# Four 32x32 transposes of beta moved up in VectorE's queue

## The chip, the cores and the metric

One Trainium2 chip, one of its cores. The metric is the device time of one execution in microseconds (us). Three runs of the kernel before took 374.45, 374.64 and 375.24 us; the median is 374.64.

## The reference

Sigmoid attention over 8 batches, 12 heads, 448 positions and 64 features per head, and behind it a feed-forward layer whose activation is `h * sigmoid(beta * h)`, with one `beta` for each of the 2048 hidden features:

```
def _attn_ref(q, k, v):
    S = q.shape[2]
    scale = 1.0 / np.sqrt(q.shape[-1])
    scores = scale * np.matmul(q, k.transpose(0, 1, 3, 2)) - np.log(S)
    attn = 1.0 / (1.0 + np.exp(-scores))
    return np.matmul(attn, v).astype(np.float32)

def _moe_ref(x, w_in, w_out, beta):
    h = x @ w_in
    g = h * (1.0 / (1.0 + np.exp(-beta * h)))
    return (g @ w_out).astype(np.float32)
```

`x` is the attention's output as 3584 rows of 768; `w_in` is 768 x 2048, `w_out` 2048 x 768. The kernel takes and gives float32 and multiplies in float16.

## The kernel before

**The steps.** A *group* is four heads of one batch, so a batch has three groups. For a group, `load_one` (L126) brings q and k into `raw`, GpSimd issuing the load; VectorE transposes 32x32 blocks into `qT` (L208) and `kT` (L217, L221). TensorE multiplies them into score tiles in PSUM (`score`, L237), and ScalarE turns a score tile into weights `attns` (L250 for one tile, L265 for two at once). TensorE multiplies the weights with `v` (`attend`, L340), and VectorE casts the result into `xT` (L349). Then comes the first layer (`dense1`, L362): six products with `w_in` make one column block `dc` of h; ScalarE takes its sigmoid with a column of `beta_sb` as scale (L374), and VectorE multiplies (L377). The second layer (L392) writes the output through `osb`. Later windows of the work use sums of blocks in Strassen's manner (L531, L651, L445); they are the same in both kernels.

**The order.** Nothing is scheduled by a planner: the program's order is each engine's order. The first 50 us are written out by hand in the list `BEGIN`, and each engine takes its own instructions out of that list in their order:

- `("q", g, half)` and `("k", g)`: VectorE's transposes of group g (a half of q is 224 of the 448 positions).
- `("scores", g, half, second)`: the scores of group g for one half of the queries (`half_visit`). `second` 0 takes key tiles 0 and 1, `second` 1 the rest. Each entry is 16 products on TensorE into two score tiles, and behind them two activations on ScalarE.
- `("v", 0)`: a copy on VectorE (L171) of the last part of v of batch 0.
- `("values", g, half)`: 16 products (L340) and two casts (L349) for group g.
- `("dense", n)`: the next n products of the list `fill`, here products of the first layer for batch 0.
- `("idle", n)`: n products of zeros (L820) whose result nobody reads.
- `("beta",)`: `beta_columns`, four transposes on VectorE (L834) that turn the sixteen rows of 128 in `beta_in` into columns in `beta_sb`. SyncE loads `beta_in` (L822) at the start, behind a memset on VectorE (L815).

**Score tiles.** At first there are three score tiles, each of two PSUM banks (`share_psum(3)`), and they are taken in turn, two for an entry. Counted from the first entry of scores, tile numbers are 0 1, 2 0, 1 2, 0 1, 2 0, 1 2, 0 1, 2 0, 1 2; after `("two",)` there are two tiles. Where `second` is 0, the order of the 16 products is: two into the first tile, two into the second, and so on. So the third product of `("scores", 0, 1, 0)`, which is the seventh entry and has tiles 0 and 1, needs tile 1 to be free, and tile 1 was filled last by `("scores", 2, 0, 1)`, whose first activation empties it.

```
        def beta_columns():
            ready.add("beta")
            for i in range(P // BLK):
                part = slice(i * BLK, (i + 1) * BLK)
                nc.vector.transpose(out=beta_sb[part], in_=beta_in[:, part])
```

Of the kernel before, what the change touches and what calls it, by code (L numbers as in the profile page):

```python
# [13 lines left out]
def kernel(  # L14
# [70 lines left out]
    def bank(cols: int = S, hold=None, at=None):  # L85
        if at is None:
            at = min((i for i in used if i not in held.values()), key=used.get)
        assert at not in held.values()
        touch(at)
        if hold is not None:  # L90
            held[hold] = at
        width[at] = cols
        return ps[:, at, 0:cols]
# [669 lines left out]
    with tc.manual_schedule():  # L763
# [52 lines left out]
        idle = bank(512)  # L816
# [13 lines left out]
        def beta_columns():  # L830
# [5 lines left out]
        BEGIN = [  # L836
            ("cast", 1, 0, 8, False), ("cast", 1, 8, 14, True), ("cast", 0, 0, 7, True), ("k", 0), ("q", 0, 0),
            ("q", 1, 0), ("idle", 20), ("scores", 0, 0, 1), ("k", 1), ("idle", 1), ("idle", 4), ("idle", 2),
            ("k", 2), ("q", 2, 0), ("scores", 1, 0, 0), ("idle", 9), ("v", 0), ("scores", 1, 0, 1),
            ("scores", 0, 0, 0), ("idle", 7), ("scores", 2, 0, 0), ("values", 0, 0), ("q", 1, 1),  # L840
            ("scores", 2, 0, 1), ("beta",), ("q", 0, 1), ("values", 1, 0), ("scores", 0, 1, 0),
            ("values", 2, 0), ("scores", 0, 1, 1), ("dense", 6), ("scores", 1, 1, 1), ("two",), ("dense", 9),
            ("loads",), ("scores", 1, 1, 0), ("q", 2, 1), ("dense", 21), ("scores", 2, 1, 0), ("dense", 12),
            ("values", 0, 1), ("scores", 2, 1, 1), ("values", 1, 1), ("values", 2, 1), ("dense", 45), ("k", 3),
# [182 lines left out]
```

## Time and profile before

| | |
|---|---|
| median of three runs | 374.64 us (374.45 to 375.24) |
| the profiled execution | 374.53 us, of which its span is 372.8 us |
| TensorE busy | 366.1 us, 98% of the span |
| ScalarE busy | 260.0 us, 70% |
| VectorE busy | 254.4 us, 68% |
| GpSimd busy | 90.4 us, 24% |
| granted TensorE clock, mean | 0.999 |

The profile is of one execution. Times in it are us from the span's start, of which 1.73 us of the execution lie outside (374.53 less 372.8). In a row of the timeline the columns are start, duration, engine, line, operation, result and operands with their shapes, the count of merged instructions, and in brackets the engine's idle time before them with the one that ended it. Merged rows hold instructions that overlap a little, so a sum of means can exceed a row's duration. PE is TensorE, DVE is VectorE, ACT is ScalarE, POOL is GpSimd, SP is SyncE, and PEld is TensorE's loading of weights.

### The profile page before, as it was taken

The numbers are of one execution on the slowest core, as the hardware profiler recorded it, in microseconds if no ns is written. First come the engines' busy times: TensorE is split into PE (matmuls) and PEld (weight loads), VectorE is DVE, ScalarE is ACT, GpSimd is POOL, SyncE is SP. The second block draws the span as 40 slices with busy tenths as digits, with TensorE's granted clock in tenths as the row PEclk, the third lists the DMA queues.
The fourth block names the chain that finished last, engine by engine and source line by source line (L and its number), as shares of the span: only waits on it lengthen the run. The fifth ranks groups of instructions, "written<-read, shape, count | busy, mean of one in ns | idle before, by whom it ended". The sixth has DMA issues, their size and how long they took to land.

```text
span 372.8 us, 7315 instructions
## 1 busy us (share of the span) xinstructions
PE 366.1 (98%) x2907; PEld 185.1 (50%) x2907; DVE 254.4 (68%) x479; ACT 260.0 (70%) x311; POOL 90.4 (24%) x136
## 2 busy tenths in 40 slices
PE   8899999999999999999999999999999999999996
PEld 5466544443444455544444445554444455555664
DVE  4335786776586966787666767778767667679671
ACT  5995766698967668887777749887678647883000
POOL 7833343141151013234133003235100002230000
PEclk9999999999999999999999999999999999999999
DMA  9999999993369030029829410018903111000333
GB/s 171 177 195 203 198 204 198 218 124 51 51 85 174 1 86 1 2 49 128 165 38 218 103 24 21 3 30 113 164 4 86 42 44 42 3 0 1 86 84 128
DMA packets 42546, 34.65 MB, mean 93 GB/s; under 512 B 21888, under 2 KB 38928, under 8 KB 42512
## 3 DMA queue, kind: packets, MB, share of 16 engines
q0 software_dynamic: 36688, 22.47, 44.5%
q1 hardware_dynamic: 5824, 11.71, 10.9%
q8 instruction: 23, 0.38, 0.4%
q14 instruction: 11, 0.09, 0.1%
HBM read 45.62 MB, written 11.01 MB: 152 GB/s over the span
## 4 chain that ended last, share of the span: by engine, by line
PE 89%; ACT 5%; DVE 2%; DMA 1%; issue 1%; POOL 0%; ACTq 0%; POOLq 0%
PE ps L531 26%; PE ps L651 25%; PE ps L237 11%; PE ps L340 10%; PE ps L362 9%; PE ps L392 4%; PE ps L445 4%; ACT attns L265 2%; ACT attns L250 2%; DMA raw<-in_k_dram 1%; ACT sg L374 1%; DVE xT L349 0%; DVE qT L208 0%; DVE kT L217 0%; ACT osb L672 0%
## 5 line engine op out<-in xcount | busy, mean ns | idle before, releaser
L265 ACT ACTIVATE attns<-ps,nlogs 128x1792 f16<-128x1792 f32 x75 | 131.7, 1756 | 41.1 <-PE ps L237 40.1
L651 PEld LDWEIGHTS <-sum 128*128 128x128 f16 x440 | 40.4, 98 | 37.0 <-issue 12.1
L545 POOL TENSOR_TENSOR gt<-attns,sg 128x448 f16<-128x448 f32 x21 | 23.9, 1139 | 141.6 <-ACT sg L542 141.6
L237 PE MATMUL ps<-qT,kT 32*128 32x448 f16 (+3 forms) x864 | 52.3, 341 | 2.1 <-ACT attns L250 1.1
L542 ACT ACTIVATE sg<-ps,beta_sb 128x448 f32<-128x448 f32 x72 | 45.3, 633 | 8.4 <-PE ps L531 5.9
L531 PE MATMUL ps<-xT,w_in 128*128 128x448 f16 x216 | 49.2, 353 | 0.0
L531 PE MATMUL ps<-xT,w_S 128*128 128x448 f16 x216 | 49.2, 352 | 0.0
L651 PE MATMUL ps<-w_T,sum 128*128 128x384 f16 x264 | 48.5, 327 | 0.0
L545 DVE TENSOR_TENSOR gt<-ps,sg 128x448 f16<-128x448 f32 x72 | 44.3, 619 | 3.9 <-ACT sg L542 3.7
L349 DVE CAST xT<-ps 128x448 f16<-128x448 f32 (+1 forms) x54 | 28.9, 568 | 19.8 <-PE ps L340 19.8
L531 PEld LDWEIGHTS <-w_in 128*128 128x128 f16 x288 | 28.0, 98 | 26.6 <-issue 0.7
L340 PE MATMUL ps<-attns,v 128*64 128x448 f16 (+3 forms) x432 | 40.6, 340 | 0.1
L669 DVE TENSOR_TENSOR osb<-ps,osb 128x384 f32<-128x384 f32 x55 | 30.5, 555 | 14.4 <-PE ps L651 12.6
L362 PE MATMUL ps<-xT,w_in 128*128 128x448 f16 (+1 forms) x240 | 39.8, 316 | 0.1
L638 DVE TENSOR_TENSOR sum<-gt 128x1024 f16<-128x1024 f16 x55 | 36.5, 680 | 0.2
L377 DVE TENSOR_TENSOR gt<-ps,sg 128x448 f16<-128x448 f32 (+1 forms) x40 | 20.0, 528 | 22.6 <-ACT sg L374 22.5
L126 POOL DMA_DIRECT2D raw<-in_q_dram x26 | 14.5, 560 | 81.0 <-DVE kT L221 75.1
L651 PE MATMUL ps<-w_out,gt 128*128 128x384 f16 x176 | 33.4, 327 | 0.0
L651 PE MATMUL ps<-w_out,sum 128*128 128x384 f16 x176 | 32.2, 327 | 0.0
L591 DVE TENSOR_TENSOR ps<-ps,attns 128x448 f32<-128x448 f32 x24 | 15.2, 633 | 23.3 <-PE ps L531 20.0
L531 PEld LDWEIGHTS <-w_S 128*128 128x128 f16 x216 | 21.1, 98 | 19.4
L362 PEld LDWEIGHTS <-w_in 128*128 128x128 f16 x240 | 21.9, 98 | 16.8 <-issue 5.6
(54 smaller groups left out, 377.0 us busy)
## 6 DMA issues: line engine op xcount, KB each, us to landing
out_dram<-osb SPq DMA_DIRECT2D x100, 96.0 KB, 2.2
raw<-in_k_dram POOLq DMA_DIRECT2D x23, 224.0 KB, 5.6
raw<-in_q_dram POOLq DMA_DIRECT2D x21, 224.0 KB, 3.8
v<-in_v_dram POOLq DMA_DIRECT2D x32, 144.0 KB, 6.2
w_in<-in_moe_w_in_dram POOLq DMA_DIRECT2D x8, 384.0 KB, 10.4
w_out<-in_moe_w_out_dram POOLq DMA_DIRECT2D x4, 768.0 KB, 13.8
v<-in_v_dram POOLq DMA_DIRECT2D x16, 48.0 KB, 6.1
out_dram<-osb SPq DMA_DIRECT2D x2, 384.0 KB, 2.3
```

The source lines that it names most:

```text
L237: nc.tensor.matmul(sco[base : base + nk, hh, u0 : u0 + n], kT[g][lo : lo + BLK, jt * P : jt * P + nk, e], qT[g][lo : lo + BLK, c0 : c0 + n ...
L265: nc.scalar.activation(out=attns[:, slot : slot + 2].rearrange("p n h s -> p (n h) s"), in_=sco, func=AF.Sigmoid, bias=nlogs[:, 0:1], scal ...
L340: nc.tensor.matmul(av[hh * D : (hh + 1) * D, 0:n], vs[b][base : base + nk, 2 * (s % NPAIR) + hh, jt], at[base : base + nk, hh, 0:n], start ...
L349: nc.vector.tensor_copy(out=xTs[b][:, s % NPAIR, c0 : c0 + n], in_=av[:, 0:n])
L362: nc.tensor.matmul(m1, w_in16[:, hc, dc * P : (dc + 1) * P], xTs[b][:, hc, c0 : c0 + n], start=(hc == 0), stop=(hc == NHC - 1),)
L377: nc.vector.tensor_tensor(out=gt[:, dc, off : off + n], in0=m1, in1=sg[:, 0:n], op=ALU.mult)
L531: nc.tensor.matmul(out, w[:, c, i * P : (i + 1) * P], m[:, c], start=(start and c == 0), stop=(c == KH - 1), skip_group_check=not start,)
L542: nc.scalar.activation(out=sg, in_=h, func=AF.Sigmoid, bias=0.0, scale=beta_sb[:, dc : dc + 1])
L545: return lambda: engine.tensor_tensor(out=gt[:, dc, b % 2 * S : b % 2 * S + S], in0=h, in1=sg, op=ALU.mult)
L638: nc.vector.tensor_tensor(out=sums[t, i], in0=x, in1=y, op=op)
L651: nc.tensor.matmul(m2, (x if op is None else sums[t, i])[:, dc], w[:, dc], start=first, stop=(dc == ND - 1), skip_group_check=i >= 4,)
L669: nc.vector.tensor_tensor(out=out, in0=in0, in1=in1, op=op)
```

## The change

One entry of the list moves. `("beta",)` stood behind the second scores of group 2, between the transposes `("q", 1, 1)` and `("q", 0, 1)` in VectorE's order. It now stands behind the first scores of group 1; in VectorE's order that is behind `("q", 2, 0)` and ahead of the copy `("v", 0)`. No instruction is added or removed, and the order on TensorE, ScalarE, GpSimd and SyncE is the same.

```
         BEGIN = [
...
-            ("k", 2), ("q", 2, 0), ("scores", 1, 0, 0), ("idle", 9), ("v", 0), ("scores", 1, 0, 1),
+            ("k", 2), ("q", 2, 0), ("scores", 1, 0, 0), ("beta",), ("idle", 9), ("v", 0), ("scores", 1, 0, 1),
             ("scores", 0, 0, 0), ("idle", 7), ("scores", 2, 0, 0), ("values", 0, 0), ("q", 1, 1),
-            ("scores", 2, 0, 1), ("beta",), ("q", 0, 1), ("values", 1, 0), ("scores", 0, 1, 0),
+            ("scores", 2, 0, 1), ("q", 0, 1), ("values", 1, 0), ("scores", 0, 1, 0),
             ("values", 2, 0), ("scores", 0, 1, 1), ("dense", 6), ("scores", 1, 1, 1), ("two",), ("dense", 9),
...
```

More of the change, by code (lines that the diff above doesn't have):

```diff
@@ L838 @@
             ("q", 1, 0), ("idle", 20), ("scores", 0, 0, 1), ("k", 1), ("idle", 1), ("idle", 4), ("idle", 2),
-            ("k", 2), ("q", 2, 0), ("scores", 1, 0, 0), ("idle", 9), ("v", 0), ("scores", 1, 0, 1),
+            ("k", 2), ("q", 2, 0), ("scores", 1, 0, 0), ("beta",), ("idle", 9), ("v", 0), ("scores", 1, 0, 1),
             ("scores", 0, 0, 0), ("idle", 7), ("scores", 2, 0, 0), ("values", 0, 0), ("q", 1, 1),
-            ("scores", 2, 0, 1), ("beta",), ("q", 0, 1), ("values", 1, 0), ("scores", 0, 1, 0),
+            ("scores", 2, 0, 1), ("q", 0, 1), ("values", 1, 0), ("scores", 0, 1, 0),
             ("values", 2, 0), ("scores", 0, 1, 1), ("dense", 6), ("scores", 1, 1, 1), ("two",), ("dense", 9),
```

## The prediction

> **What bounds the kernel now.** I read the page first, then busy time by stretches, the waits of TensorE, and then the chain of waits around the moved instructions.
>
> ```profile
> span 372.8 us, 7315 instructions
> PE 366.1 (98%) x2907; PEld 185.1 (50%) x2907; DVE 254.4 (68%) x479; ACT 260.0 (70%) x311; POOL 90.4 (24%) x136
> ...
> 13.50:17.00 3.50, 3.04 (x58) 1.73 (x56) 2.57 (x10) 3.50 (x5) 3.50 (x6) 1.00 1.38 182
> ...
> 45.00:100.00 55.00, 55.00 (x471) 23.88 (x464) 39.60 (x69) 44.19 (x38) 16.00 (x28) 1.00 0.93 149
> ...
> PE ps L820 <- DVE still L814: 1.2, 1, 1.2
> PE ps L237 <- ACT attns L250: 1.1, 3, 0.6
> PE ps L237 <- DVE qT L208: 0.5, 1, 0.5
> PE ps L237 <- DVE kT L217: 0.3, 1, 0.3
> ```
>
> In the stretches the columns behind the length are busy PE, PEld, DVE, ACT, POOL, then the granted clock. TensorE is the bound: busy for 98% of the span, and for 55.00 of 55.00 us from 45 to 100. At the start it is ScalarE's turn: from 13.5 to 17 ACT is busy for all 3.50 us and PE for 3.04. So a microsecond won there counts at the end only if it makes ScalarE, and TensorE behind it, earlier; later, with TensorE full, only a transfer or its own order could take it back. The last four rows are the whole list of waits of TensorE's products (us in total, times, longest): it waits once for a transposed q, for 0.5 us, and for no transfer. The chain of waits shows where:
>
> ```profile
> 15.39 0.32 DVE qT L208
> 15.71 0.08 DVE beta_sb L834
> ...
> 16.23 0.20 DVE beta_sb L834
> ...
> 16.47 0.42 DVE qT L208
> ...
> 16.94 0.63 PE ps L237 x16
> 17.57 1.80 ACT attns L250 x2
> ```
>
> The transposes of beta stand on the chain that ended last, ahead of a q that TensorE wants. That q is `("q", 0, 1)`, and the waiting products are `("scores", 0, 1, 0)`.
>
> **The change part by part: what goes.** VectorE's and TensorE's own rows around that place:
>
> ```profile
> 9.17 0.37 DVE L208 STREAM_TRANSPOSE qT<-raw 128x224 f32<-128x224 f32 x1
> 13.49 0.35 DVE L171 COPY v<-v 64x768 f16<-64x768 f16 x1 [3.95 <-DMA v<-in_v_dram]
> ...
> 15.31 0.40 DVE L208 STREAM_TRANSPOSE qT<-raw 128x224 f32<-128x224 f32 x1
> 15.63 0.80 DVE L834 STREAM_TRANSPOSE beta_sb<-beta_in 32x32 f32<-32x32 f32 x4
> 16.47 0.41 DVE L208 STREAM_TRANSPOSE qT<-raw 128x224 f32<-128x224 f32 x1
> 16.80 0.65 DVE L349 CAST xT<-ps 128x224 f16<-128x224 f32 x2
> ...
> 15.49 0.98 PE L340 MATMUL ps<-attns,v 128*64 128x224 f16 x16
> 16.94 0.58 PE L237 MATMUL ps<-qT,kT 32*128 32x224 f16 x16 [0.46 <-DVE qT L208]
> ```
>
> Without beta the transpose of q can start at 15.63, behind the one of 15.31, instead of 16.47: 0.84 us earlier, done at 16.04. But TensorE is busy with `("values", 1, 0)` until 15.49 + 0.98 = 16.47, so of the 0.84 us at most its own wait of 0.46 is to be had.
>
> Is the q there by 15.63, and what is late next? The load's issue (GpSimd, with the us to landing from the list of issues for that moment), and ScalarE's rows:
>
> ```profile
> 10.13 0.53 POOL L126 DMA_DIRECT2D raw<-in_q_dram  x1 [0.21 <-issue]
> raw<-in_q_dram POOLq DMA_DIRECT2D x1, 112.0 KB, 4.7
> ...
> 10.42 1.01 ACT L250 ACTIVATE attns<-ps,nlogs 128x896 f16<-128x896 f32 x1
> 11.48 0.57 PE L237 MATMUL ps<-qT,kT 32*128 32x224 f16 x14 [0.63 <-ACT attns L250]
> ...
> 15.62 1.53 ACT L250 ACTIVATE attns<-ps,nlogs 128x896 f16<-128x896 f32 x2
> 16.52 0.63 ACT L250 ACTIVATE attns<-ps,nlogs 128x448 f16<-128x448 f32 x1
> 17.55 3.41 ACT L250 ACTIVATE attns<-ps,nlogs 128x896 f16<-128x896 f32 x4 [0.40 <-PE ps L237]
> ```
>
> The q lands at 10.13 + 4.7 = 14.83, 0.80 ahead of 15.63. Next to be late is the score tile. The third product of the entry needs the tile that the activation of 15.62 empties. The pattern is seen once whole in this stage: the activation of 10.42 ends at 11.43, and 14 products, all but the two that fitted the free tile, start 0.05 later and take 0.57. An activation of the same size from 15.62 ends at 15.62 + 1.01 = 16.63, so the 14 start at 16.68 and are done at 17.25. Before, they were done at 16.94 + 0.58 = 17.52. That is **0.27 us earlier**, not 0.46. ScalarE is free at 16.52 + 0.63 = 17.15, so its next activation moves from 17.55 to 17.28, and 0.13 of its idle 0.40 stays.
>
> The bounds of this term: 0.46 if the tile comes free for nothing, zero if something else stops TensorE there. I take 0.27, because the row of 11.48 is the same wait on the same kind of tile.
>
> From 17.28 on the stage is a relay between ScalarE and TensorE. The next products to wait for a tile are those of `("scores", 1, 1, 1)`:
>
> ```profile
> 20.48 0.70 PE L237 MATMUL ps<-qT,kT 32*128 32x224 f16 x14 [0.29 <-ACT attns L250]
> ```
>
> They wait for an activation of the same unbroken ScalarE row that began at 17.55, so they move by the same 0.27. The two casts, at 16.80 only since they stood behind q, go back to about 16.5, so the PSUM banks of `("values", 2, 0)` come free in time for its start at about 17.2.
>
> **What is added.** The four transposes now start behind the q of 9.17, at 9.54, and end at 9.54 + 0.84 = 10.38. Behind them in VectorE's queue is the copy of v, which waits for its own load until 13.49: 3.11 us of cover. Four instructions in idle time are costed at nothing; without that cover they would cost 0.84. The wait that moves with them is for `beta_in`:
>
> ```profile
> 1.65 0.43 SPq L822 DMA_DIRECT2D beta_in<-in_moe_beta_dram  x1
> ...
> beta_in<-in_moe_beta_dram SPq DMA_DIRECT2D x1, 8.0 KB, 4.0
> ```
>
> It lands at 5.65, 3.89 us before its new use. Queued behind it are the copy of v, the casts of values and two transposes of q; who waits for these is TensorE with `("values", 0, 0)` from 13.57. No DMA moves in any queue.
>
> **GpSimd beside it.** In their new place the transposes run while GpSimd issues loads (10.13, then eight of `w_in` from 11.13).
>
> ```profile
> 11.13 6.58 POOL L177 DMA_DIRECT2D w_in<-in_moe_w_in_dram  x8 [0.47 <-DMA v<-in_v_dram]
> ...
> L177 POOL DMA_DIRECT2D w_in<-in_moe_w_in_dram x8: 828/844/871, 11.1 to 16.8; - x8
> ```
>
> In the old place they ran beside the issues of `w_in`, and the longest of the eight took 871 ns against a median of 844: no hold is to be seen, so I cost nothing; held for all of the transposes, the issue of 10.13 would start at 10.38 instead, q land at 15.08, and the sum stay. The Trainium skill ("SBUF — State Buffer", SBUF: two separate sides) says that VectorE and GpSimd share a pair of SBUF ports, that an instruction of VectorE which takes both locks GpSimd out of writing DMA descriptors, and that an issue of some 620 ns took some 3100 ns beside such a copy. By that figure, as an estimate, the issue would end 2.48 us later and the sum would be a loss of 0.84 us (rival C) instead of a gain of 0.27.
>
> **Does the 0.27 us arrive?** Then TensorE needs `w_in` 0.27 us sooner. GpSimd's waits show when parts of it landed at the latest:
>
> ```profile
> 19.66 0.55 POOL L126 DMA_DIRECT2D raw<-in_k_dram  x1 [1.40 <-DMA w_in<-in_moe_w_in_dram]
> ...
> 23.69 0.88 POOL L185 DMA_DIRECT2D w_out<-in_moe_w_out_dram  x1 [1.14 <-DMA w_in<-in_moe_w_in_dram]
> ...
> 21.11 1.11 PE L362 MATMUL ps<-xT,w_in 128*128 128x224 f16 x9
> ...
> 25.57 1.31 PE L362 MATMUL ps<-xT,w_in 128*128 128x224 f16 x12
> ```
>
> The second load (column blocks 2 and 3) is there by 19.66 and first used after six of the nine products of 21.11, so at 21.11 + 6/9 of 1.11 = 21.85; the fourth (blocks 6 and 7) is there by 23.69 and used at 25.57. Both have about 2 us. Sum: nothing added, 0.27 gone: 374.53 - 0.27 = 374.26 us against the profiled execution. That execution is 0.11 below the median of the three runs, so against the median it is 374.64 - 0.27 = **374.37, say 374.4 us**, 0.07% faster. About 0.2%, 0.75 us, is what a measurement of this kernel can tell from no change, so I forecast "within".
>
> **The rivals.**
>
> A. The whole of beta comes off the path. The chain of waits carries it by name, and VectorE's part of it is 16.47 - 15.63 = 0.84 us: 374.53 - 0.84 = 373.69, faster by 0.22%. For it: the ends of TensorE's products are modelled, so the 16.47 at which it is free, and with it the cap of 0.46, is less sure than VectorE's rows. Against it: the activation of 16.52 ends at 17.15, so ScalarE, which is full from 13.5, can't win over 0.40. Chance 0.23.
>
> B. Nothing arrives: the gain is swallowed on the way, by a tile, a bank or a transfer that is as late as before. 374.5. Against it stand the 2 us of `w_in` and the unbroken ScalarE row. Chance 0.13.
>
> C. The transposes hold GpSimd back at 10.13. The q of 15.63 lands late by the hold. Up to 0.80 us that costs nothing, and at 16.47 - 14.83 = 1.64 us all is as before; from there each us costs one. Slower by over 0.75 us needs a hold of 2.39, three times the four transposes; a hold of 2.48 gives 374.53 + 0.84 = 375.37. The page of the Trainium skill named above is the ground for such a size; the eight issues of `w_in` that lay beside the same instructions don't bear it out. Chance 0.07.
>
> D. On the slower side by the moved wait: beta's load is late in the executions that are timed. The place is VectorE's queue ahead of the copy of v; it decides from a landing at 13.49 - 0.84 = 12.65, 7.0 us later than here, and then costs one for one.
>
> ```profile
> w_out<-in_moe_w_out_dram POOLq DMA_DIRECT2D x4, 768.0 KB, 13.8
> ```
>
> If it took as long as the loads of `w_out`, it would land at 1.65 + 13.8 = 15.45, 2.80 too late: 374.53 + 2.80 = 377.3. Against it: it is 8 KB against 768. Chance 0.07.
>
> **How the numbers follow.** The forecast has 0.50, B 0.13 and both lie within 0.2%, less 0.02 for a gain that a measurement lifts over the limit: same 0.61. A, with those 0.02: faster 0.25. C and D: slower 0.14. The range goes down to A, 373.69, and a little under it for the 0.08 us by which the lowest run lies under the profiled one: 373.6. Up it goes to B as the highest of the three runs had it, 375.24: 375.3. C and D, 0.14, lie outside.
>
> **What would show it.** In the changed kernel the four rows of L834 start near 9.5 with no idle time ahead of them; the copy of v stays at 13.49; the q of 16.47 starts at 15.63; TensorE's wait for L208 of 0.5 is gone, and in its place stands a wait of about 0.2 for ACT L250; the ScalarE row of 17.55 starts near 17.28 with 0.13 idle ahead of it; every later row up to 100 us is 0.27 earlier. I am wrong if the first products behind `("values", 1, 0)` wait for something else, if the copy of v is later than 13.5, if the issue of 10.13 takes much over 0.53, or if the rows are 0.27 earlier at 20 and not at 45.

## The result and the profile after

The changed kernel took 374.39 us (median of 21 runs, 374.07 to 375.37); the kernel before, in 21 runs beside it, 375.03 us (374.41 to 376.85). The ratio is 0.9983 with a 95% interval of 0.9975 to 0.9990: faster by 0.17%. The profiled execution took 374.09 us, its span 372.3 us; the one profiled before took 0.44 us more (374.53).

VectorE's and TensorE's timelines of the changed kernel around the moved instructions:

```profile
9.64 0.81 DVE L834 STREAM_TRANSPOSE beta_sb<-beta_in 32x32 f32<-32x32 f32 x4
13.72 0.35 DVE L171 COPY v<-v 64x768 f16<-64x768 f16 x1 [3.27 <-DMA v<-in_v_dram]
14.65 0.69 DVE L349 CAST xT<-ps 128x224 f16<-128x224 f32 x2 [0.58 <-PE ps L340]
15.26 0.69 DVE L208 STREAM_TRANSPOSE qT<-raw 128x224 f32<-128x224 f32 x2
16.46 0.69 DVE L349 CAST xT<-ps 128x224 f16<-128x224 f32 x2 [0.51 <-PE ps L340]
...
15.44 0.99 PE L340 MATMUL ps<-attns,v 128*64 128x224 f16 x16
16.36 0.84 PE L237 MATMUL ps<-qT,kT 32*128 32x224 f16 x16
17.13 0.99 PE L340 MATMUL ps<-attns,v 128*64 128x224 f16 x16
```

Beta runs where VectorE had nothing to do, the two transposes of q stand together, and TensorE's wait for the second is gone. Before, the held products started at 16.94; now they start at 16.36, as soon as the values ahead of them are issued. ScalarE's timelines show what that is worth, the kernel before first and then the changed one:

```profile
8.62 8.54 ACT L250 ACTIVATE attns<-ps,nlogs 128x896 f16<-128x896 f32 x10 [0.29 <-PE ps L237]
```

```profile
8.57 11.99 ACT L250 ACTIVATE attns<-ps,nlogs 128x896 f16<-128x896 f32 x14 [0.43 <-PE ps L237]
20.45 0.45 ACT L374 ACTIVATE sg<-ps,beta_sb 128x224 f32<-128x224 f32 x1
```

One row of 14 activations where there were rows of 10 and 4 with 0.40 us between them (the row of 4 is that of 17.55 in the prediction). And the stretches of TensorE show that the gain is carried along (columns as before):

```profile
13.50:17.00 3.50, 3.50 (x67) 2.07 (x64) 2.19 (x7) 3.50 (x5) 3.47 (x6) 1.00 1.38 185
45.00:100.00 55.00, 55.00 (x465) 23.94 (x464) 39.31 (x69) 44.16 (x38) 16.10 (x28) 1.00 0.92 149
```

From 13.5 to 17 TensorE is now full as well, and from 45 to 100 it was and is full, so nothing takes the gain back. The last products, in the timelines of the kernel before and of the changed one:

```profile
368.70 0.82 PE L445 MATMUL ps<-w_out,sum 128*128 128x192 f16 x8
```

```profile
368.27 0.82 PE L445 MATMUL ps<-w_out,sum 128*128 128x192 f16 x8
```

They start 0.43 us earlier. Of this, 0.05 has nothing to do with beta: ScalarE's long row started at 8.57 instead of 8.62. Two lengths that leave the start out serve as rulers from here on. **Ruler 1** goes from the start of ScalarE's first activation behind the k of group 1 (8.62, 8.57) to the first activation of the held entry, `("scores", 0, 1, 0)` (17.55, 17.15): 8.93 us before, 8.58 after, so **0.35 us**. **Ruler 2** goes from the same start to the start of the last row of products: 360.08 before, 359.70 after, so 0.38.

### The profile page after: what moved, and what is told of

Read it like the earlier page. It is cut to its first block, busy times and chain, and to the rows that moved or that the text cites. A ratio compares the mean times of both kernels' runs of the same rounds, so it can differ in the third digit from the quotient of the medians.

```text
span 372.3 us, 7315 instructions
## 1 busy us (share of the span) xinstructions
PE 364.9 (98%) x2907; PEld 184.7 (50%) x2907; DVE 254.2 (68%) x479; ACT 259.7 (70%) x311; POOL 90.6 (24%) x136
## 4 chain that ended last, share of the span: by engine, by line
PE 90%; ACT 5%; DMA 1%; issue 1%; DVE 1%; POOL 0%; ACTq 0%; POOLq 0%
PE ps L531 26%; PE ps L651 25%; PE ps L237 11%; PE ps L340 10%; PE ps L362 9%; PE ps L392 4%; PE ps L445 4%; ACT attns L265 2%; ACT attns L250 2%; DMA raw<-in_k_dram 1%; ACT sg L374 1%; DVE kT L217 0%; ACT osb L672 0%; PE ps L820 0%; DVE w_in L491 0%
## 5 line engine op out<-in xcount | busy, mean ns | idle before, releaser
L377 DVE TENSOR_TENSOR gt<-ps,sg 128x448 f16<-128x448 f32 (+1 forms) x40 | 19.9, 527 | 22.5 <-ACT sg L374 22.4
```

What stands on the lines that cost most here:

```text
L377: nc.vector.tensor_tensor(out=gt[:, dc, off : off + n], in0=m1, in1=sg[:, 0:n], op=ALU.mult)
```

## The experiments

Theory H: ahead of q, beta held TensorE and through it ScalarE; the gain is that hold, capped by the 0.40 us that ScalarE had idle there. Rivals: the timed difference (0.64 us between the medians) comes in part from the start (S); the gain depends on the empty place that takes the transposes (P); GpSimd is held there (C); the hold counts one for one from the first transpose on (A).

### The same change, timed again

The changed kernel as it is, 12 runs, beside 35 of the kernel before; the next three experiments were timed beside the same 35.

> The changed kernel as it is, beside the others on one chip. Theory H (the hold): beta ahead of q held TensorE, and with it ScalarE, for 0.35 us; the time is 0.35 us (0.09%) under before, and ScalarE's row is unbroken from 8.6 to 20.5. Rival S (start): part of the 0.64 us between the medians comes from how the first loads happen to land, not from the moved instructions; then the difference on this chip is well off 0.35 in either direction and the profile still shows 0.35 between the rows of 16 and of 18.

374.77 us against 375.04, 0.27 us less, ratio 0.9988 (0.9977 to 0.9998). The span was 373.4 us, 1.1 longer than that of the first profile of the very same program, and longer than the kernel before had. ScalarE's timeline, and VectorE's of the same profile:

```profile
9.65 11.99 ACT L250 ACTIVATE attns<-ps,nlogs 128x896 f16<-128x896 f32 x14 [1.50 <-PE ps L237]
18.23 1.01 ACT L250 ACTIVATE attns<-ps,nlogs 128x896 f16<-128x896 f32 x1
...
8.40 0.58 DVE L217 STREAM_TRANSPOSE kT<-raw 128x384 f32<-128x384 f32 x1 [1.54 <-DMA raw<-in_k_dram]
```

The k of group 1 could be transposed at 8.40 instead of 7.32, since its load landed later, and all behind it is later by as much: ScalarE's long row starts 1.25 us behind it in both (8.57 - 7.32, 9.65 - 8.40). Ruler 1 gives 18.23 - 9.65 = 8.58, ruler 2 369.34 - 9.65 = 359.69: the same program to 0.01 us. So S is right that the start moves a run by more than the change does, and the instructions behind the start are worth the same in both: the change itself is 0.35 to 0.38 us (0.10%). That the rest of the 0.64, and the gap from 0.64 to 0.27, is how the first loads happened to land is likely but not shown: only one run of each set has a trace. 0.10% lies inside the second interval and on the edge of the first.

### Beta behind q instead of far ahead

```
-            ("scores", 2, 0, 1), ("beta",), ("q", 0, 1), ("values", 1, 0), ("scores", 0, 1, 0),
+            ("scores", 2, 0, 1), ("q", 0, 1), ("beta",), ("values", 1, 0), ("scores", 0, 1, 0),
```

(against the kernel before)

> The four transposes stand one place further down than in before: behind the transpose of q's second half instead of ahead of it, and so ahead of the casts of the values of group 1. Theory H: q starts at about 15.6, TensorE's wait for it is gone, ScalarE's idle 0.40 is gone; the casts start near 16.8 as in before, which cost nothing there; 0.35 us faster than before, the same as the changed kernel. Rival P (the place): the gain comes from the empty stretch of VectorE from 9.5 to 13.5 that takes the work; then this order, which leaves all 0.84 us in the busy stretch, gains nothing or the late casts hold the products behind them, up to 0.3 us.

374.70 us, ratio 0.9986 (0.9977 to 0.9996). VectorE's timeline:

```profile
16.26 0.69 DVE L208 STREAM_TRANSPOSE qT<-raw 128x224 f32<-128x224 f32 x2
16.88 0.81 DVE L834 STREAM_TRANSPOSE beta_sb<-beta_in 32x32 f32<-32x32 f32 x4
17.72 0.69 DVE L349 CAST xT<-ps 128x224 f16<-128x224 f32 x2
```

Ruler 1 gives 8.59, ruler 2 359.70. One place further down does what the long way up did. P falls: what counts is that q is not behind beta. The casts come late, and no row of TensorE there waits for them.

### Beta twice, at the old place and at the new one

The entry `("beta",)` doubled, once in the kernel before and once in the changed kernel; the second set writes the same columns.

> The four transposes are run twice at the old place (the second time over the same columns). Theory H: no cover is left there, so the second set costs one for one: q starts at about 17.3, the wait for it grows from 0.46 to about 1.3, 0.84 us (0.22%) slower than before. Rival B (swallowed later): ScalarE or a transfer gives part of it back; under 0.4 us slower.

> The four transposes are run twice at the new place. Theory H: 1.65 us of the 3.3 us that VectorE still has to wait there for v; nothing moves: equal to the changed kernel within noise, 0.35 us under before. Rival C (GpSimd held): transposes beside the issue of loads hold it; the issue of the load of q at 10.3 is later or longer by some tenths, and w_in with it.

At the old place 376.35 us, ratio 1.0028 (1.0016 to 1.0040); at the new one 374.86 us, 0.9996 (0.9983 to 1.0008). The timing of the second says little by itself; its profile is clear. TensorE at the old place, then GpSimd and VectorE at the new one:

```profile
18.26 0.58 PE L237 MATMUL ps<-qT,kT 32*128 32x224 f16 x16 [1.45 <-DVE qT L208]
```

```profile
11.00 0.53 POOL L126 DMA_DIRECT2D raw<-in_q_dram  x1 [0.20 <-issue]
11.78 6.59 POOL L177 DMA_DIRECT2D w_in<-in_moe_w_in_dram  x8 [0.25 <-DMA v<-in_v_dram]
...
10.35 1.79 DVE L834 STREAM_TRANSPOSE beta_sb<-beta_in 32x32 f32<-32x32 f32 x8
14.32 0.35 DVE L171 COPY v<-v 64x768 f16<-64x768 f16 x1 [2.19 <-DMA v<-in_v_dram]
```

At the old place the wait grows by 0.99 us, from 0.46 to 1.45, and ruler 2 by 0.94, from 360.08 to 361.02: nearly all of the second set is on the path, and it costs 0.94 where 0.84 was expected. Its rival, under 0.4 us, falls. At the new place ruler 2 stays at 359.70, and 2.19 us of cover are left. C falls too: with eight transposes from 10.35 to 12.14 beside it, the issue of q's load at 11.00 takes 0.53 us and the eight of `w_in` 6.59, as without them.

### Some of the four left at the old place

The helper takes a range of the four, and the entry is split between the two places: two and two, then one at the new place and three left.

```
-            for i in range(P // BLK):
+            for i in range(lo, hi):
```

> Two of the four transposes at the new place, two left ahead of q at the old. Read on ScalarE from the start of its first activation behind the k of group 1 (8.62 in before) to the first activation of the held entry (17.55): 8.93 us in before, 8.58 in the changed kernel. Theory H with its cap: q is done 0.42 us sooner than in before, just ahead of the tile's release, so nearly the whole gain is there already: 8.58 to 8.63. Rival A (one for one): half of the gain, 8.75.

> One transpose at the new place, three left ahead of q. Theory H with its cap: q is late now by itself, one transpose (0.21 us) less late than in before: 8.93 - 0.21 = 8.72 on the same stretch. Rival A (one for one in quarters of the 0.35): 8.84.

Each was run once. With two left the span was 372.5 us and ruler 1 17.37 - 8.71 = 8.66, a little over H's 8.58 to 8.63 and under A's 8.75. With three left, 373.0 us and ruler 1 17.86 - 8.98 = 8.88, where H had said 8.72 and A 8.84: H missed by 0.16, A by 0.04. VectorE's timeline with three left shows why:

```profile
15.67 0.40 DVE L208 STREAM_TRANSPOSE qT<-raw 128x224 f32<-128x224 f32 x1
16.11 0.63 DVE L834 STREAM_TRANSPOSE beta_sb<-beta_in 32x32 f32<-32x32 f32 x3
16.77 0.41 DVE L208 STREAM_TRANSPOSE qT<-raw 128x224 f32<-128x224 f32 x1
```

From one transpose of q to the next it takes 16.77 - 15.67 = 1.10 us with three between them, and took 16.47 - 15.31 = 1.16 with four. The one taken away, which writes partitions 0 to 31, had cost only 0.06 us, not a quarter of 0.84. Before, it started at 15.63, ahead of the end of the q at 15.71; the next three never start ahead of the end of what precedes them (here 16.11, behind 16.07). The Trainium skill ("VectorE: DVE Perf Modes", Two Vector instructions with no wait between them) says that an instruction whose input or output starts in another group of 32 partitions than the last one's in the same memory is held till all earlier ones have finished. The three that write partitions 32, 64 and 96 behave so here.

Against q's real lateness both runs fit H, though H had its price per transpose wrong. Counted from the start of ScalarE's row, q started at 16.47 - 8.62 = 7.85 before, 16.77 - 8.98 = 7.79 with three left and 16.29 - 8.71 = 7.58 with two left: 0.06 and 0.27 sooner, for 0.05 and 0.27 on ruler 1. In the changed kernel q starts at 15.26 + 0.69 - 0.41 = 15.54, which is 0.88 sooner by the same count, for 0.35. So up to 0.27 the hold counts one for one in q's start, and by 0.88 it has stopped at 0.35; no run lies between. A is right up to that cap and wrong in its sum.

### Past the cover

The entry at the new place six times, 24 transposes, in one run.

> The four transposes are run six times at the new place, 24 in place of 4: some 5.4 us where VectorE has 4.1 us before the load of v lets it go on. Theory H (cover): the copy of v comes 1.2 us late, the last products of the first values with it, and ScalarE's row breaks some 0.6 to 1.1 us; the transposes are free only as far as the cover reaches. Rival (the place is free): no break, 8.58 as in the changed kernel.

Span 373.3 us. VectorE, TensorE, ScalarE:

```profile
9.67 5.53 DVE L834 STREAM_TRANSPOSE beta_sb<-beta_in 32x32 f32<-32x32 f32 x24
15.23 0.35 DVE L171 COPY v<-v 64x768 f16<-64x768 f16 x1
...
15.64 0.28 PE L340 MATMUL ps<-attns,v 64*64 64x224 f16 x2 [0.75 <-DVE v L171]
...
16.61 4.99 ACT L250 ACTIVATE attns<-ps,nlogs 128x896 f16<-128x896 f32 x6 [0.67 <-PE ps L237]
```

The copy of v no longer waits for its load but for the transposes, the values wait 0.75 us for it, ScalarE breaks for 0.67, and ruler 2 is 369.29 - 8.84 = 360.45, 0.75 over the changed kernel. The transposes are free as far as the wait for v reaches.

### Can the start be made quiet?

In every profile so far ScalarE's long row starts 1.25 us behind the first transpose of the k of group 1, whenever that can start (7.32 to 8.40), and the rest follows. Two ways to loosen that, on the changed kernel. First, that load issued ahead of q's (and transposed ahead of it):

```
-            ("q", 1, 0), ("k", 1), ("k", 2), ("q", 2, 0), ("v", 0, 3), ("last",), ("q", 1, 1), ("q", 2, 1),
+            ("k", 1), ("q", 1, 0), ("k", 2), ("q", 2, 0), ("v", 0, 3), ("last",), ("q", 1, 1), ("q", 2, 1),
```

> The changed kernel with the load of k of group 1 issued ahead of that of q's first half, and VectorE's transposes of the two in that order too. In the profiles so far TensorE's first scores of group 1 start between 7.96 and 9.04, just behind the landing of that k, and the end of the span follows them one for one. Theory L (landing): k lands some 0.5 us sooner, the scores start near 8.0 whatever the landing, the runs lie closer together and the median is 0.3 to 0.8 us under the changed kernel. Rival (bandwidth): both loads share the same DMA engines and the later of the two lands when it did; no gain, or a loss of up to 0.4 us since q is now the last.

374.56 us (373.86 to 376.03), ratio 0.9991 (0.9976 to 1.0005). k was transposed at 6.75, but the scores waited for q and began at 8.00. The 0.3 to 0.8 us under the changed kernel did not come, nor did the runs lie closer together. The profile fits the rival, since q was now the last to come; the interval holds both no change and the changed kernel's gain, so whether the order costs anything stays open.

Second, other work first. The second scores of group 0 need nothing that is late:

```
-            ("k", 2), ("q", 2, 0), ("scores", 1, 0, 0), ("beta",), ("idle", 9), ("v", 0), ("scores", 1, 0, 1),
-            ("scores", 0, 0, 0), ("idle", 7), ("scores", 2, 0, 0), ("values", 0, 0), ("q", 1, 1),
+            ("k", 2), ("q", 2, 0), ("scores", 0, 0, 0), ("beta",), ("idle", 9), ("v", 0), ("scores", 1, 0, 0),
+            ("scores", 1, 0, 1), ("idle", 7), ("scores", 2, 0, 0), ("values", 0, 0), ("q", 1, 1),
```

> The changed kernel with the second scores of group 0, whose q and k are there already, ahead of both scores of group 1. ScalarE waits for the k of group 1 between 0.43 and 1.5 us in the profiles so far, and the end of the span follows that landing one for one. Theory L (landing): the two activations of group 0 (1.8 us) fill that wait, the span no longer follows the landing, and the runs are 0.4 to 1.2 us under the changed kernel. Rival (next late): the copy of v, which waits for its load until 13.5 to 14.3, stands next and the first values wait for it; 0 to 0.3 us gained.

**373.80 us (373.36 to 373.97), ratio 0.9974 (0.9965 to 0.9984)**: faster than the kernel before, and the 9 runs lie within 0.61 us where 27 of the kernel before beside them spread over 1.26. Against the changed kernel it is not decided: that was not timed beside it, and its two intervals (0.9975 to 0.9990, 0.9977 to 0.9998) overlap with this one. ScalarE's and VectorE's timelines:

```profile
6.77 13.66 ACT L250 ACTIVATE attns<-ps,nlogs 128x896 f16<-128x896 f32 x16 [1.63 <-PE ps L237]
...
7.95 0.58 DVE L217 STREAM_TRANSPOSE kT<-raw 128x384 f32<-128x384 f32 x1 [1.75 <-DMA raw<-in_k_dram]
```

k came 0.63 us later than in the changed kernel's first profile (7.95 against 7.32), and the last products still start earlier (368.14 against 368.27): in this profile ScalarE no longer breaks for it.

A third order went further and put each of the first three values one entry later:

> The same, with each of the first three values one entry of scores later, so that the copy of v is wanted some 1.7 us later. Theory L: if the load of v is what is late in the run before this, this order gains what that one could not, 0.4 to 1.2 us under the changed kernel in all. Rival: values later leave the score tiles without weights to free and ScalarE breaks behind them; no better than the run before.

374.59 us, ratio 1.0000 (0.9991 to 1.0009). No gain, and for a reason that neither theory nor rival had. ScalarE's row of 16 stayed whole, but the first layer stood right behind the last of those values and waited for its cast, in TensorE's timeline:

```profile
20.17 0.74 PE L362 MATMUL ps<-xT,w_in 128*128 128x224 f16 x6 [0.48 <-DVE xT L349]
```

And on the changed kernel, work was moved into the wait of 0.29 us near 20:

```
-            ("values", 2, 0), ("scores", 0, 1, 1), ("dense", 6), ("scores", 1, 1, 1), ("two",), ("dense", 9),
+            ("values", 2, 0), ("scores", 0, 1, 1), ("dense", 9), ("scores", 1, 1, 1), ("two",), ("dense", 8),
...
-            ("loads",), ("scores", 1, 1, 0), ("q", 2, 1), ("dense", 21), ("scores", 2, 1, 0), ("dense", 12),
+            ("loads",), ("scores", 1, 1, 0), ("q", 2, 1), ("dense", 19), ("scores", 2, 1, 0), ("dense", 12),
```

> The changed kernel with three products of the first layer moved ahead of the first scores that wait 0.29 us for a tile near 20 us (9, 8 and 19 products where 6, 9 and 21 stood). From ScalarE's first activation behind the k of group 1 to the end of the span: 363.73 us in the changed kernel. Theory (TensorE is the bound from here): the wait of 0.29 is filled with work that is wanted anyway, 0.1 to 0.2 us less. Rival: ScalarE's row is the bound till 22 and the wait only moves; 363.7.

374.30 us, ratio 0.9996 (0.9986 to 1.0005); from ScalarE's start at 8.67 to the last row of products at 368.35 it is 359.68, where the changed kernel has 359.70. The wait moved (TensorE waited 0.20 and 0.18 us for VectorE's L377 instead), as its rival had it.

### Beta's hold on the quiet start

The order of the best run with beta back at its old place.

> The order of e9 (the second scores of group 0 ahead of both of group 1) with beta back at its old place, ahead of q. In e9 ScalarE's row was unbroken from 6.77 and its runs lay within 0.61 us, since nothing waits for the first landing any more. Theory H: the hold is the same on this quieter base; ScalarE breaks once, ahead of the held entry, by some 0.4 us, and the runs are 0.35 us over e9's ratio to before: 0.9974 + 0.0009 = 0.9983, with the same narrow spread. Rival: beta's hold and the landing cover each other; the ratio is e9's 0.9974.

374.14 us (373.96 to 375.01), ratio 0.9979 (0.9969 to 0.9989); by the medians' ratios 0.05% over the run without the hold, inside both intervals, and timed on another chip. The spread is not the narrow one that was expected: 1.05 us, of which one run at 375.01 makes the most, where the 13 runs of the kernel before beside it spread over 0.68. So the quiet runs of the experiment before did not come again here. The profile has the break back:

```profile
17.22 3.40 ACT L250 ACTIVATE attns<-ps,nlogs 128x896 f16<-128x896 f32 x4 [0.38 <-PE ps L237]
```

So the landing and the hold are different waits: ScalarE's row is whole over the first and breaks at the second. That the two gains add in the time is not shown.

## Why the prediction was right, and where not

**The time and the class.** 374.37 was forecast and 374.39 measured, within the 0.2% as forecast. The agreement to 0.02 is luck: the median of before had moved from 374.64 in three runs to 375.03 in 21. The forecast of the difference was 0.27 us; the medians gave 0.64 and, timed again, 0.27, the traces 0.35 to 0.39 both times. The right figure for the change is the trace's, since the runs carry the landing of a load.

**What goes.** The place, the wait of 0.46 and the landing of q ahead of its new start were right. So were the steps that most of the 0.84 us lies beside TensorE's values and that the score tile is late next. The mis-sized term is what that tile leaves: 0.27 was put where 0.35 was measured. I had ScalarE start when all of the 14 products behind the tile's release are done, at 17.28, with 0.13 us idle left. But ScalarE's next activation needs the first tile only, and the last product into that is the 14th of the 16. The row of 11.48, from which I took the pattern, has ScalarE's answer in the kernel before:

```profile
12.01 1.01 ACT L250 ACTIVATE attns<-ps,nlogs 128x896 f16<-128x896 f32 x1
```

That is 12.01 - 11.48 = 0.53 us behind the start of the 14, and not 0.57 and the 0.03 that I had added. From 16.68 it gives 17.21, 0.34 earlier than 17.55. The chain of waits of the changed kernel shows the same step:

```profile
16.43 0.70 PE ps L237 x14
17.13 0.02 issue
17.15 1.82 ACT attns L250 x2
```

There the two products into the free tile start at 16.36, ahead of the values' modelled end of 15.44 + 0.99 = 16.43. The other 14 go on at 16.62, 0.04 behind the activation that empties their tile (15.57 + 1.01 = 16.58), and ScalarE starts at 17.15, again 0.53 later. Its last activation had ended at 16.47 + 0.63 = 17.10, so 0.05 of the idle 0.40 stayed, and 0.35 went. The wait of about 0.2 for L250 that I had expected on TensorE does not appear as a wait here, since the two early products cover it.

**What is added.** Cost at nothing, and it was: 3.27 us of wait for v remained behind the four transposes. The runs with 8 and 24 show how far that reaches. The copy of v came at 13.72, later than the 13.5 that was named as a sign of being wrong; it waited for its load and not for the transposes, so the sign was badly chosen.

**GpSimd and rival C.** No hold: in the changed kernel the issue of q's load, now at 10.32, takes 0.53 as before, with the last of the transposes beside it until 9.64 + 0.81 = 10.45.

**Does it arrive.** Yes; ruler 2 shows 0.38 at the end of what ruler 1 shows as 0.35 at 17 us. Where the 0.03 more comes from was not followed up.

**The rivals.** A's price of 0.84 was wrong, but the argument against it, that ScalarE can't win over 0.40, was the nearest bound of all, and I should have asked how much of the 0.40 could go. B did not happen, nor did D: the transposes start at 9.64 with no wait for beta. What no rival named is the start, which moved two profiles of the same program by 1.1 us.

## What to carry to other kernels

A small instruction in an in-order queue costs what stands behind it: ask what the next instruction in that queue feeds, and move the small one to either side of that, even by one place. Before crediting a difference of a few tenths to an edit, measure it in the profile from an event behind the first loads, not from the span's start. And where an engine waits at the start for a load that lands at varying times, try work ahead of that wait whose data are there: here it filled the wait and was faster than the kernel before, though its gain over the changed kernel is not decided.

## What had not been expected of the hardware

The same load, issued at 2.00 to 2.01 us, let the k of group 1 be transposed at 7.37, 7.32, 8.40, 8.32, 7.71 and 8.27 in the profiles of the kernel before, the changed one and the first four experiments, in none of which its queue was changed ahead of it. That is over 1 us between executions, three times the effect under study. And a 32x32 transpose of 0.16 to 0.20 us cost what stood behind it from 0.06 us (the first, on the partitions where the output of the instruction ahead of it starts) to 0.24 us (the mean of one set of four more, 0.94).
